# The last V ahead of wo, wo in five loads through four column tiles, K's pairs in one loop, one store

## The chip, the cores and the metric

The kernel runs on one core of a Trainium2 chip. The core has a matrix engine (PE; its weight loads are listed as PEld), a vector engine (DVE), a scalar engine (ACT), GpSimd (POOL) and a sync engine (SP) that here only issues transfers. Sixteen DMA engines move data between the chip's memory (DRAM) and the on-chip buffer; SP's loads stand in one queue, in the order in which SP issues them. The metric is the device time of one execution in microseconds; the time of a kernel is the median of its runs.

## What is computed

One step of a decoder for one token: attention over a long cache, a small feed-forward net, and a gate that mixes the two.

```python
q = (x @ wq).reshape(B, Sq, H, Dh)            # B = Sq = 1, D = 512, H = 32, Dh = 128
scores = einsum("bhqd,bhkd->bhqk", q, k_cache) * Dh ** -0.5      # Sk = 65536
p = softmax(scores, axis=-1)
o = einsum("bhqk,bhkd->bhqd", p, v_cache)
a = o.reshape(B, Sq, H * Dh) @ wo             # wo: 4096 x 512
b = (silu(x @ w_gate) * (x @ w_up)) @ w_down  # F = 1792
out = g * a + (1 - g) * b                     # g = sigmoid(sum(x * gate_w))
```

All tensors are bf16. K and V are 32 heads x 65536 positions x 128, 537 MB each; they are read once. wo is 4.2 MB.

## The kernel before

**Storage.** One buffer `mem` has 184 KB per partition, addressed in KB by `at(kb, n)`. A head's K and V come in halves z = 0 and 1 (in the load calls 0 and 1, in the names `a` and `z`) of 64 KB per partition, 8.39 MB each. K's first half lies at 32 to 96, its second at 0 to 64; V's first at 120 to 184, its second at 96 to 160. Halves overlap, so a half can be loaded when parts of the others have been used up. That is what the semaphores `ktdone` (pieces of K transposed by DVE) and `pvdone` (groups of value matmuls finished by PE) tell SP.

**The loop over heads.** DVE transposes K in sixteen pieces per head into two alternating buffers `kt` (lines 322, 415, 422). PE scores each piece against q with 32 small matmuls (`scores`, line 472), which are grouped in pairs of pieces, one for each buffer. The score row goes through a maximum (336, 547, 338, 549) and an exponential on ACT (288), and DVE puts it in the layout `pb` that the value matmuls need (331). One head behind, PE multiplies V by `pb` with 128 matmuls of 512 columns (line 525), in four groups: (0,0) with 40, (0,1) with 24, (1,0) with 40, (1,1) with 24. `psO` collects the head's row in 4 x 512; ACT scales it (280) and `turn()` brings it into a column (499), which ACT puts into `oTn` (282).

In one pass of the loop PE's order is: three pairs of K's first half in an inner loop, value group (0,0), the fourth pair written out, the turn of the last row, group (0,1), four pairs of K's second half, group (1,0), the maximum, group (1,1). SP's order is the next K first half, V first half, K second half, V second half, each behind a wait (lines 241 to 249). V's second half waits for group (0,0) (line 248).

**The end.** The last head's V isn't multiplied in the loop. After the last pass SP loads 31 of wo's 32 row blocks (line 251), then the last V in eight pieces (the list `tail`: place, first row, rows; a row is 128 x 128 values), then the block that is left twice: `wj` in the layout of the other blocks and `w31` with head 31's own rows (lines 260 and 261). PE multiplies the pieces of V as weights with a column of `pb` (`piece`, line 561, one matmul for each row, into a column `psW`). Between the first piece and the second, DVE has put the 31 finished heads into `amat`, one matmul (571) gathers them in wo's row order into `oR`, and 31 matmuls of 512 columns (576) add them to `psY`, which already holds the feed-forward branch. `psY` is copied to a row (440) and spread over `psZ` (584). When the last piece is done, DVE scales `psW` (442) and eight matmuls (600) add what is left, through two column tiles of two rows each. ACT copies the result (300), and ACT and SP store one half each.

Of the kernel before, what the change touches and what calls it, by code (L numbers as in the profile page):

```python
# [5 lines left out]
P = 128  # L6
KB = 512
PR = 32
# [13 lines left out]
def bass_gated_mix__mha_block_cached__swiglu_ffn__decode_kernel(  # L22
# [38 lines left out]
    tail = [(32, 0, 128), (0, 128, 128), (V0 + 24, 256, 128), (V0 + 64, 384, 64),  # L61
            (V0 + 80, 448, 32), (V0 + 56, 480, 16), (V0 + 60, 496, 12), (V0 + 63, 508, 4)]
    WOJ, WO31 = V0, V0 + 1

    with ExitStack() as ctx:
# [28 lines left out]
        hot = sb("hot", [P, 2, 2], F32)  # L94
# [10 lines left out]
        oR = sb("oR", [P, 32], BF16)  # L105
        w4 = sb("w4", [P, 2, 2, 2], BF16)
# [14 lines left out]
        names = ("x", "gw", "wq", "wg", "wu", "wd", "ka0", "ka", "kz", "va", "vz", "wo", "wj", "w31")  # L121
        d = {n: sem("d_" + n) for n in names}
        dt_ = [sem(f"d_t{i}") for i in range(len(tail))]
        s_ones = sem("s_ones")
# [6 lines left out]
        s_hot0 = sem("s_hot0")  # L131
        s_hot = sem("s_hot")
# [35 lines left out]
        s_oR = sem("s_oR")  # L168
        s_y = sem("s_y")
        s_yr = sem("s_yr")  # L170
        s_w = sem("s_w")
        s_w4 = sem("s_w4")
        s_wj = sem("s_wj")
# [3 lines left out]
        s_out2 = sem("s_out2")  # L177
# [12 lines left out]
        wj_dram = w_dram["wo"][:, 31 * D:32 * D]  # L190
        w31_dram = A_wo.rearrange("(h d) n -> h d n", d=Dh)[H - 1]
        WQ, WG, WU, WD, WO = V0, 0, 14, V0 + 64, 64
# [4 lines left out]
        wo_ap = at(WO, 32 * D).rearrange("p (j n) -> p j n", j=32)  # L197
        w2_ap = at(WOJ, 2 * D).rearrange("p (e c n) -> p e c n", e=2, c=4)
# [18 lines left out]
        ctx.callback(lambda: nc.sync.wait_ge(s_out2, 16))  # L217
        block = ctx.enter_context(nc.Block())

        @block.sync  # L220
        def _(sp):
            def load(kind, h, z):
                cache = A_k_cache if kind == "k" else A_v_cache
                sp.dma_start(at(place(kind, h, z), HR * Dh), kv_dram(cache, h)[z]).then_inc(d[kind + "az"[z]], 16)  # L224
# [12 lines left out]
            sp.wait_ge(ktdone, 2 * NP + NP // 2)  # L237
            load("k", 1, 1)
            sp.wait_ge(pvdone, 5)
            load("v", 0, 1)  # L240
            with nc.sync.Fori(0, H - 2) as i:
                sp.wait_ge(ktdone, i * (2 * NP) + (4 * NP - 4))
                load("k", i + 2, 0)
                sp.wait_ge(pvdone, i * 4 + 7)
                load("v", i + 1, 0)
                sp.wait_ge(ktdone, i * (2 * NP) + (4 * NP + NP // 2))
                load("k", i + 2, 1)
                sp.wait_ge(pvdone, i * 4 + 9)
                load("v", i + 1, 1)
            sp.wait_ge(ktdone, 2 * NP * H - NP)  # L250
            sp.dma_start(at(WO, 31 * D), w_dram["wo"][:, 0:31 * D]).then_inc(d["wo"], 16)
# [11 lines left out]
            sp.dma_start(out_dram[2:4, :], fin[32:34, :]).then_inc(s_out2, 16)  # L263

        @block.scalar
        def _(act):
# [31 lines left out]
            row_norm(H - 2)  # L298
            act.wait_ge(s_z4, 1)
            nc.scalar.copy(fin[0:34, :], psZ[0:34, 0:128]).then_inc(s_fin, 1)  # L300
            act.wait_ge(s_fin, 1)
            act.dma_start(out_dram[0:2, :], fin[0:2, :]).then_inc(s_out, 16)

        @block.vector
        def _(dve):
# [45 lines left out]
            link(nc.vector.memset(w4[:], 0.0))  # L351
            nc.vector.memset(psZ[0:64, 0:128], 0.0).then_inc(s_zz, 1)
            nc.vector.memset(hot[0:1, :, :], 0.0)
# [7 lines left out]
            nc.vector.memset(hot[0:1, :, :].rearrange("p a b -> p (a b)")[:, 0:4:3], 1.0).then_inc(s_hot, 1)  # L361
# [74 lines left out]
            nc.vector.tensor_copy(oR[:], psQ[:, 0, 0:32]).then_inc(s_oR, 1)  # L436
            diag = w4[:].rearrange("p e a b -> p e (a b)")[:, :, 0:4:3]
            nc.vector.tensor_copy(diag[:, 0, :], psQ[:, 0, 31:32].to_broadcast([P, 2])).then_inc(s_wj, 1)
            dve.wait_ge(s_y, 1)
            nc.vector.tensor_copy(yrow[0:1, :], psY[0:1, :]).then_inc(s_yr, 1)  # L440
            dve.wait_ge(s_w, 1)
            nc.vector.tensor_scalar(diag[:, 1, :], psW[:, 0:1].to_broadcast([P, 2]), LiG, None, ALU.mult).then_inc(s_w4, 1)

        @block.tensor
        def _(pe):
# [22 lines left out]
            def scores(b, col, j):  # L468
                for r in range(NG):
                    for je in range(4):  # L470
                        o = col + PR * b + 4 * r
                        last = nc.tensor.matmul(psS[:, o:o + 4] if j is None else psS[:, ds(j * (2 * PR) + o, 4)],  # L472
# [18 lines left out]
            for j in range(FC):  # L491
                last = nc.tensor.matmul(psY[0:1, :], guT[:, j:j + 1], wd_ap[:, j, :],
                                        start=(j == 0), stop=False)
# [3 lines left out]
            def turn():  # L497
                for i in range(4):
                    last = nc.tensor.matmul(psT[:, 0:1], orow[0:4, i * Dh:(i + 1) * Dh], ident[0:4, i:i + 1],  # L499
                                            start=(i == 0), stop=(i == 3))  # L500
                last.then_inc(s_pt, 1)

            nc.tensor.sem_inc(pvdone, 4)
            with nc.tensor.Fori(0, H) as i:
                n = i * (2 * NP)

                def pair(c, j):
                    for b in range(2):
                        if c == 0 and b == 0:
                            pe.wait_ge(s_qc, i + 1)  # L510
                        pe.wait_ge(ktdone, n + (c + b + 1) if j is None else n + j * 2 + (c + b + 1))
                        scores(b, PR * c, j)

                def pieces(z, c0, c1):
                    if c1 - c0 == 2:
                        pair(NP * z + c0, None)
                        return
                    with nc.tensor.Fori(0, (c1 - c0) // 2) as j:
                        pair(NP * z + c0, j)
# [11 lines left out]
                pieces(0, 0, NP - 2)  # L531
# [23 lines left out]
            def piece(n):  # L555
# [3 lines left out]
                for r in range(nr):  # L559
                    col = k_col[r0 + r]  # L560
                    last = nc.tensor.matmul(psW[:, 0:1], vt[:, r * Dh:(r + 1) * Dh], pb[:, col:col + 1],  # L561
                                            start=(r0 + r == 0), stop=(r0 + r == R - 1))
# [3 lines left out]
            turn()  # L566
            pe.wait_ge(s_pba, H)
            piece(0)
# [4 lines left out]
            pe.wait_ge(s_oR, 1)  # L573
            pe.wait_ge(d["wo"], 16)
            for j in range(31):
                last = nc.tensor.matmul(psY[0:1, :], oR[:, j:j + 1], wo_ap[:, j, :], start=False, stop=(j == 30))
            last.then_inc(s_y, 1)
            piece(1)
            pe.wait_ge(s_yr, 1)
            pe.wait_ge(s_hot, 1)  # L580
            pe.wait_ge(s_zz, 1)
            zt = [psZ[32 * (c // 2):32 * (c // 2) + 2, 0:128] for c in range(4)]
            for c in (0, 2, 1, 3):
                nc.tensor.matmul(zt[c], hot[0:1, c % 2, :], yrow[0:1, 128 * c:128 * c + 128],
                                 start=(c % 2 == 0), stop=False)
            pe.wait_ge(s_pbz, H)
            piece(2)
            piece(3)
            piece(4)
            piece(5)  # L590
            piece(6)
            piece(7).then_inc(s_w, 1)
            pe.wait_ge(s_wj, 1)
            pe.wait_ge(d["wj"], 16)
            for e in range(2):
                if e == 1:
                    pe.wait_ge(d["w31"], 16)
                    pe.wait_ge(s_w4, 1)
                for c in (0, 2, 1, 3):
                    last = nc.tensor.matmul(zt[c], w4[:, e, c % 2, :], w2_ap[:, e, c, :], start=False,  # L600
                                            stop=(e == 1 and c % 2 == 1))
# [29 lines left out]
```

## Time and profile before

| | us |
|---|---|
| median of 3 runs | 2513.8 (2513.74 to 2513.82) |
| span of the profiled execution | 2512.4 |
| PE busy | 1709.8 |
| DVE busy | 1411.8 |
| ACT busy | 64.6 |
| moved from DRAM | 1087.77 MB, 433 GB/s over the span |

The span is the time from the first to the last instruction of one profiled execution; the runs' times also hold what lies around it. A row of the timeline has the start in us from the start of the span, the length, engine, line, operation, output and inputs with their sizes, how many instructions are merged, and in brackets the idle time of that engine just before and what ended it. SPq and ACTq rows are the instructions that issue transfers. "Granted clock" is the matrix engine's clock as a share of its full speed.

### The profile page before, as it was taken

The page shows a single profiled execution, that of the slowest core. Times are in us where ns is not written, and L with a number is a line of the kernel's source. Part 1 is how long each engine was busy: PE and PEld are TensorE (multiplying, and loading weights), DVE is VectorE, ACT ScalarE, POOL GpSimd, SP SyncE. Part 2 cuts the span into 40 slices and gives each one's busy share as a digit, 9 for nine tenths or more (in the row PEclk, how much of TensorE's full clock was granted, in tenths as well). Part 3 has the DMA queues.
Part 4 walks back from the last instruction along what each step waited for, and adds up shares of the span by engine and source line. Part 5 has one row for each costly group of instructions (what it writes and reads, how often), then busy time and mean ns, then how long its engine had stood idle before and what let it go on. Part 6 is the DMA issues. An engine that isn't in the chain of part 4 may idle for free.

```text
span 2512.4 us, 51694 instructions
## 1 busy us (share of the span) xinstructions
PE 1709.8 (68%) x21624; PEld 978.8 (39%) x21624; DVE 1411.8 (56%) x1683; ACT 64.6 (3%) x195; POOL 0.2 (0%) x4
## 2 busy tenths in 40 slices
PE   4666766667667677676676766766767767677677
PEld 3334433333433344333443333343334333344334
DVE  4764565554655645646456555465564564645653
ACT  0000000000000000000000000000000000000000
POOL 0000000000000000000000000000000000000000
PEclk8667767777677677776776767767767677677677
DMA  9999999999999999999999999999999999999999
GB/s 420 436 434 434 434 435 434 434 434 434 434 434 434 434 434 434 434 434 434 434 434 434 434 434 434 434 434 434 434 434 434 434 434 434 435 434 434 434 435 402
DMA packets 20470, 1087.93 MB, mean 433 GB/s; under 512 B 2282, under 2 KB 2668, under 8 KB 2924
## 3 DMA queue, kind: packets, MB, share of 16 engines
q1 hardware_dynamic: 20452, 1087.78, 100.0%
q8 instruction: 9, 0.15, 0.0%
q14 instruction: 1, 0.01, 0.0%
q10 hardware_dynamic: 8, 0.00, 0.0%
HBM read 1087.77 MB, written 0.00 MB: 433 GB/s over the span
## 4 chain that ended last, share of the span: by engine, by line
DMA 70%; PE 27%; DVE 1%; issue 1%; SPq 0%; ACT 0%; DVEq 0%
DMA mem<-in_A_v_cache_dram 67%; PE psO L525 27%; DMA mem<-in_A_k_cache_dram 2%; DMA mem<-in_A_wo_dram 1%; DVE kt L322 1%; DMA mem<-in_A_wq_dram 0%; DVE kt L415 0%; SPq L224 0%; PE psM L456 0%; DVE pb L331 0%; PE psS L472 0%; PE psM L547 0%; DVE sm L336 0%; PE psZ L600 0%; PE psM L549 0%
## 5 line engine op out<-in xcount | busy, mean ns | idle before, releaser
L472 PE MATMUL psS<-qcur,kt 128*128 128x4 bf16 x16384 | 573.0, 169 | 728.3 <-DVE kt L415 414.2
L525 PE MATMUL psO<-mem,pb 128*4 128x512 bf16 x3968 | 1040.6, 428 | 32.9 <-DMA mem<-in_A_v_cache_dram 32.6
L472 PEld LDWEIGHTS psS<-qcur,kt 128*128 128x128 bf16 x16384 | 534.0, 105 | 791.9 <-issue 789.5
L422 DVE STREAM_TRANSPOSE kt<-mem 128x2048 uint32<-128x2048 uint32 x248 | 547.6, 2275 | 402.3 <-DMA mem<-in_A_k_cache_dram 402.3
L415 DVE STREAM_TRANSPOSE kt<-mem 128x2048 uint32<-128x2048 uint32 x248 | 551.3, 2280 | 240.3 <-DMA mem<-in_A_k_cache_dram 239.3
L525 PEld LDWEIGHTS psO<-mem,pb 128*4 128x4 bf16 x3968 | 359.4, 93 | 657.5 <-issue 238.4
L331 DVE COPY pb<-pa 32x64 bf16<-32x64 bf16 x1024 | 233.5, 228 | 15.1 <-ACT pa L288 1.5
L338 DVE TENSOR_REDUCE sc<-psM 1x1 f32<-1x128 f32 x32 | 8.9, 279 | 334.9 <-PE psM L547 334.9
L336 DVE TENSOR_REDUCE sm<-psS 128x1 f32<-128x512 f32 x32 | 22.1, 692 | 42.3 <-PE psS L472 42.3
L322 DVE STREAM_TRANSPOSE kt<-mem 128x2048 uint32<-128x2048 uint32 x16 | 35.4, 2277 | 17.0 <-DMA mem<-in_A_k_cache_dram 17.0
L286 ACT ACTIVATE sm<-psM 128x1 f32<-128x1 f32 x32 | 5.5, 171 | 1222.7 <-PE psM L549 1222.7
L282 ACT ACTIVATE oTn<-psT,gcol 128x1 f32 (+1 forms) x31 | 8.2, 264 | 1035.1 <-PE psT L499 1035.1
L499 PE MATMUL psT<-ident,orow 4*128 4x1 f32 x256 | 33.5, 248 | 0.5 <-ACT orow L280 0.5
L499 PEld LDWEIGHTS psT<-ident,orow 4*128 4x128 f32 x256 | 30.8, 186 | 1.2 <-ACT orow L280 0.6
L280 ACT ACTIVATE orow<-psO,sm 4x512 f32<-4x512 f32 x31 | 21.0, 677 | 130.3 <-PE psO L525 126.0
L288 ACT ACTIVATE pa<-psS,sm 128x512 bf16<-128x512 f32 x32 | 22.0, 687 | 1.0
L549 PE MATMUL psM<-sc,onesf 1*128 1x1 f32 x64 | 12.3, 259 | 11.9 <-DVE sc L338 11.9
L561 PE MATMUL psW<-pb,mem 128*128 128x1 bf16 x512 | 14.5, 164 | 5.2 <-DMA mem<-in_A_v_cache_dram 4.7
L549 PEld LDWEIGHTS psM<-sc,onesf 1*128 1x128 f32 x64 | 9.6, 186 | 21.5 <-DVE sc L338 21.5
L561 PEld LDWEIGHTS psW<-pb,mem 128*128 128x128 bf16 x512 | 13.9, 100 | 6.4 <-issue 4.2
L553 PEld LDWEIGHTS psM<-sm,onesf 128*128 128x128 f32 x64 | 9.7, 191 | 14.7 <-issue 13.5
L553 PE MATMUL psM<-sm,onesf 128*128 128x1 f32 x64 | 12.5, 264 | 1.1 <-ACT pa L288 1.1
(72 smaller groups left out, 94.0 us busy)
## 6 DMA issues: line engine op xcount, KB each, us to landing
mem<-in_A_v_cache_dram SPq DMA_DIRECT2D x3, 4096.0 KB, 29.4
mem<-in_A_k_cache_dram SPq DMA_DIRECT2D x2, 4096.0 KB, 38.7
mem<-in_A_wq_dram SPq DMA_DIRECT2D x1, 4096.0 KB, 12.3
mem<-in_A_wo_dram SPq DMA_DIRECT2D x1, 3968.0 KB, 36.7
mem<-in_A_v_cache_dram SPq DMA_DIRECT2D x1, 2048.0 KB, 31.2
mem<-in_B_w_gate_dram SPq DMA_DIRECT2D x1, 1792.0 KB, 16.0
mem<-in_B_w_up_dram SPq DMA_DIRECT2D x1, 1792.0 KB, 21.0
mem<-in_B_w_down_dram SPq DMA_DIRECT2D x1, 1792.0 KB, 24.7
```

The lines of the kernel that those rows point to most:

```text
L288: nc.scalar.activation(pa[:], psS[:], ACT.Exp, bias=nbias, scale=SCALE, accum_out=rsum).then_inc(expdone, 1)
L322: nc.vector.transpose(kt[:, i % 2, :].rearrange("p (j r t) -> p r j t", j=2, t=32), src.rearrange("p (r j t) -> p r j t", j=2, t=32)).then ...
L331: last = nc.vector.tensor_copy(dst, sr)
L336: nc.vector.reduce_max(mxs, psS[:], AX_X).then_inc(s_mx, 1)
L415: nc.vector.transpose(kt[:, c % 2, :].rearrange("p (j r t) -> p r j t", j=2, t=32), src.rearrange("p (r j t) -> p r j t", j=2, t=32)).then ...
L422: nc.vector.transpose(kt[:, c % 2, :].rearrange("p (j r t) -> p r j t", j=2, t=32), src.rearrange("p (r j t) -> p r j t", j=2, t=32)).then ...
L472: last = nc.tensor.matmul(psS[:, o:o + 4] if j is None else psS[:, ds(j * (2 * PR) + o, 4)], ktb[b][:, je // 2, r, :, je % 2], qcur[:, je, ...
L499: last = nc.tensor.matmul(psT[:, 0:1], orow[0:4, i * Dh:(i + 1) * Dh], ident[0:4, i:i + 1], start=(i == 0), stop=(i == 3))
L525: last = nc.tensor.matmul(psO[0:4, :], pb[:, k_col[256 * z + r]:k_col[256 * z + r] + 4], vt[:, r * Dh:(r + 4) * Dh], start=(z == 0 and par ...
L549: nc.tensor.matmul(amx, onesf[0:1, :], gm, start=True, stop=True).then_inc(s_ar, 1)
L553: nc.tensor.matmul(Lt, onesf[:], rsum, start=True, stop=True).then_inc(s_L, 1)
L561: last = nc.tensor.matmul(psW[:, 0:1], vt[:, r * Dh:(r + 1) * Dh], pb[:, col:col + 1], start=(r0 + r == 0), stop=(r0 + r == R - 1))
```

## The change

- The last pair of K's first half joins the other three in the inner loop, so value group (0,0) follows all four pairs. The fourth pair written out separately, and the branch between, are gone.
- The last V is loaded ahead of wo, in six pieces of 128, 128, 128, 72, 32 and 24 rows. wo is loaded after it, once, in five loads of 14, 9, 5, 3 and 1 row blocks, behind the wait for the last value group.
- The first piece of the last V is multiplied as the value matmuls in the loop are: `pb` as weights, V streaming past, 32 matmuls of 512 columns into `psO`. ACT copies the row out and a second turn adds it to `psW`, ahead of the last piece.
- All 32 heads are put in `amat`, the last one by four scalings on DVE when `psW` is complete; then one matmul gathers them and DVE copies them to `w1`.
- wo is multiplied by 128 matmuls of 128 columns, four for each row block, into four rows of `psZ` at partitions 0, 32, 64 and 96. The feed-forward branch is put there first, by four matmuls.
- ACT copies 97 partitions and stores all four rows in one transfer; SP's store is gone.

```diff
-    tail = [(32, 0, 128), (0, 128, 128), (V0 + 24, 256, 128), (V0 + 64, 384, 64),
-            (V0 + 80, 448, 32), (V0 + 56, 480, 16), (V0 + 60, 496, 12), (V0 + 63, 508, 4)]
+    tail = [(64, 0, 128), (32, 128, 128), (0, 256, 128), (V0 + 64, 384, 72), (V0 + 40, 456, 32), (V0 + 48, 488, 24)]
+    wo_rows = [14, 9, 5, 3, 1]
...
-            sp.wait_ge(ktdone, 2 * NP * H - NP)
-            sp.dma_start(at(WO, 31 * D), w_dram["wo"][:, 0:31 * D]).then_inc(d["wo"], 16)
-            need = {0: (ktdone, 2 * NP * H - 4), 1: (ktdone, 2 * NP * H), 2: (pvdone, 4 * H - 1)}
+            need = {0: (ktdone, 2 * NP * H - NP), 1: (ktdone, 2 * NP * H - 4), 2: (ktdone, 2 * NP * H),
+                    3: (pvdone, 4 * H - 1)}
...
             sp.wait_ge(pvdone, 4 * H)
-            sp.dma_start(at(WOJ, D), wj_dram).then_inc(d["wj"], 16)
-            sp.dma_start(at(WO31, D), w31_dram).then_inc(d["w31"], 16)
-            sp.wait_ge(s_fin, 1)
-            sp.dma_start(out_dram[2:4, :], fin[32:34, :]).then_inc(s_out2, 16)
+            j0 = 0
+            for n, nj in enumerate(wo_rows):
+                sp.dma_start(at(WO + j0, nj * D), w_dram["wo"][:, j0 * D:(j0 + nj) * D]).then_inc(dw_[n], 16)
+                j0 += nj
...
+            act.wait_ge(s_v0, 1)
+            nc.scalar.copy(orow[0:4, :], psO[0:4, :]).then_inc(s_or, 1)
             act.wait_ge(s_z4, 1)
-            nc.scalar.copy(fin[0:34, :], psZ[0:34, 0:128]).then_inc(s_fin, 1)
+            nc.scalar.copy(fin[0:97, :], psZ[0:97, 0:128]).then_inc(s_fin, 1)
             act.wait_ge(s_fin, 1)
-            act.dma_start(out_dram[0:2, :], fin[0:2, :]).then_inc(s_out, 16)
+            act.dma_start(out_dram, fin[0:97:32, :]).then_inc(s_out, 16)
...
+            nc.vector.tensor_copy(yrow[0:1, :], psY[0:1, :]).then_inc(s_yr, 1)
+            dve.wait_ge(s_w, 1)
+            for q in range(4):
+                w = slice(32 * q, 32 * q + 32)
+                last = nc.vector.tensor_scalar(amat[w, H - 1, q:q + 1], psW[w, 0:1], LiG[w], None, ALU.mult)
             last.then_inc(s_A, 1)
             dve.wait_ge(s_R, 1)
-            nc.vector.tensor_copy(oR[:], psQ[:, 0, 0:32]).then_inc(s_oR, 1)
...
+            nc.vector.tensor_copy(w1[:], psQ[:, 0, 0:32]).then_inc(s_w4, 1)
...
-                pieces(0, 0, NP - 2)
+                pieces(0)
                 with nc.tensor.If(i > 0):
                     pe.wait_ge(s_or, i)
                     pe.wait_ge(d["va"], i * 16)
                     pe.wait_ge(s_pba, i)
                     values(0, 0)
-                pieces(0, NP - 2, NP)
-                with nc.tensor.If(i > 0):
-                    turn()
+                    turn().then_inc(s_pt, 1)
                     values(0, 1)
-                pieces(1, 0, NP)
+                pieces(1)
...
+                    if n == 0:
+                        last = nc.tensor.matmul(psO[0:4, :], pb[:, col:col + 4], vt[:, r * Dh:(r + 4) * Dh],
+                                                start=(r == 0), stop=(r == nr - 4))
...
-            piece(0)
+            piece(0).then_inc(s_v0, 1)
+            piece(1)
+            pe.wait_ge(s_yr, 1)
+            pe.wait_ge(s_zz, 1)
+            zt = [psZ[32 * c:32 * c + 1, 0:128] for c in range(4)]
+            for c in range(4):
+                nc.tensor.matmul(zt[c], onesf[0:1, 0:1], yrow[0:1, 128 * c:128 * c + 128], start=True, stop=False)
+            pe.wait_ge(s_pbz, H)
+            piece(2)
+            piece(3)
+            piece(4)
+            pe.wait_ge(s_or, H + 1)
+            turn(psW, False, False)
+            piece(5).then_inc(s_w, 1)
             pe.wait_ge(s_A, 1)
             pe.wait_ge(s_b0, 1)
             nc.tensor.matmul(psQ[:, 0, 0:32], amat[:].rearrange("p h q -> p (h q)"), bmat[:],
                              start=True, stop=True).then_inc(s_R, 1)
...
+            pe.wait_ge(s_w4, 1)
+            j0 = 0
+            for n, nj in enumerate(wo_rows):
+                pe.wait_ge(dw_[n], 16)
+                for j in range(j0, j0 + nj):
+                    for c in range(4):
+                        last = nc.tensor.matmul(zt[c], w1[:, j:j + 1], wo_ap[:, j, c, :], start=False, stop=(j == 31))
+                j0 += nj
             last.then_inc(s_z4, 1)
```

More of the change, by code (lines that the diff above doesn't have):

```diff
@@ L93, in bass_gated_mix__mha_block_cached__swiglu_ffn__decode_kernel @@
         onesf = sb("onesf", [P, 128], F32)
-        hot = sb("hot", [P, 2, 2], F32)
         sc = sb("sc", [P, 8], F32)
@@ L104, in bass_gated_mix__mha_block_cached__swiglu_ffn__decode_kernel @@
         bmat = sb("bmat", [P, 32], BF16)
-        oR = sb("oR", [P, 32], BF16)
-        w4 = sb("w4", [P, 2, 2, 2], BF16)
+        w1 = sb("w1", [P, 32], BF16)
         fin = sb("fin", [P, 128], BF16)
@@ L119, in bass_gated_mix__mha_block_cached__swiglu_ffn__decode_kernel @@
         gm = sc[0:1, 5:6]
-        names = ("x", "gw", "wq", "wg", "wu", "wd", "ka0", "ka", "kz", "va", "vz", "wo", "wj", "w31")
+        names = ("x", "gw", "wq", "wg", "wu", "wd", "ka0", "ka", "kz", "va", "vz")
         d = {n: sem("d_" + n) for n in names}
         dt_ = [sem(f"d_t{i}") for i in range(len(tail))]
+        dw_ = [sem(f"d_w{i}") for i in range(len(wo_rows))]
         s_ones = sem("s_ones")
@@ L130, in bass_gated_mix__mha_block_cached__swiglu_ffn__decode_kernel @@
         s_unit = sem("s_unit")
-        s_hot0 = sem("s_hot0")
-        s_hot = sem("s_hot")
         s_z = sem("s_z")
@@ L167, in bass_gated_mix__mha_block_cached__swiglu_ffn__decode_kernel @@
         s_R = sem("s_R")
-        s_oR = sem("s_oR")
-        s_y = sem("s_y")
         s_yr = sem("s_yr")
         s_w = sem("s_w")
+        s_v0 = sem("s_v0")
         s_w4 = sem("s_w4")
-        s_wj = sem("s_wj")
         s_z4 = sem("s_z4")
@@ L176, in bass_gated_mix__mha_block_cached__swiglu_ffn__decode_kernel @@
         s_zz = sem("s_zz")
-        s_out2 = sem("s_out2")
         s_out = sem("s_out")
@@ L189, in bass_gated_mix__mha_block_cached__swiglu_ffn__decode_kernel @@
         }
-        wj_dram = w_dram["wo"][:, 31 * D:32 * D]
-        w31_dram = A_wo.rearrange("(h d) n -> h d n", d=Dh)[H - 1]
-        WQ, WG, WU, WD, WO = V0, 0, 14, V0 + 64, 64
+        WQ, WG, WU, WD, WO = V0, 0, 14, V0 + 64, V0
         wq_ap = at(WQ, Dc * H * Dh).rearrange("p (c n) -> p c n", c=Dc)
@@ L196, in bass_gated_mix__mha_block_cached__swiglu_ffn__decode_kernel @@
         wd_ap = at(WD, FC * D).rearrange("p (c n) -> p c n", c=FC)
-        wo_ap = at(WO, 32 * D).rearrange("p (j n) -> p j n", j=32)
-        w2_ap = at(WOJ, 2 * D).rearrange("p (e c n) -> p e c n", e=2, c=4)
+        wo_ap = at(WO, 32 * D).rearrange("p (j c n) -> p j c n", j=32, c=4)
         ktb = [kt[:, b, :].bitcast(BF16).rearrange("p (j r m e) -> p j r m e", j=2, r=NG, e=2) for b in range(2)]
@@ L216, in bass_gated_mix__mha_block_cached__swiglu_ffn__decode_kernel @@
         ctx.callback(lambda: nc.scalar.wait_ge(s_out, 16))
-        ctx.callback(lambda: nc.sync.wait_ge(s_out2, 16))
         block = ctx.enter_context(nc.Block())
@@ L350, in _ @@
             link(nc.vector.memset(amat[:], 0.0))
-            link(nc.vector.memset(w4[:], 0.0))
-            nc.vector.memset(psZ[0:64, 0:128], 0.0).then_inc(s_zz, 1)
-            nc.vector.memset(hot[0:1, :, :], 0.0)
+            nc.vector.memset(psZ[:, 0:128], 0.0).then_inc(s_zz, 1)
             nc.vector.memset(ident[:], 0.0)
@@ L360, in _ @@
             link(last)
-            nc.vector.memset(hot[0:1, :, :].rearrange("p a b -> p (a b)")[:, 0:4:3], 1.0).then_inc(s_hot, 1)
             link(nc.vector.transpose(kt[:, 1, 0:1024], kt[:, 0, 0:1024]))
@@ L433, in _ @@
                 last = nc.vector.tensor_copy(amat[32 * q:32 * q + 32, 0:H - 1, q], oTn[32 * q:32 * q + 32, 0:H - 1])
+            nc.vector.tensor_copy(yrow[0:1, :], psY[0:1, :]).then_inc(s_yr, 1)
[3 more added lines that the diff above has]
+                last = nc.vector.tensor_scalar(amat[w, H - 1, q:q + 1], psW[w, 0:1], LiG[w], None, ALU.mult)
             last.then_inc(s_A, 1)
             dve.wait_ge(s_R, 1)
[L436 to L442, printed above, removed]
+            nc.vector.tensor_copy(w1[:], psQ[:, 0, 0:32]).then_inc(s_w4, 1)
         @block.tensor
@@ L471, in scores @@
                         o = col + PR * b + 4 * r
-                        last = nc.tensor.matmul(psS[:, o:o + 4] if j is None else psS[:, ds(j * (2 * PR) + o, 4)],
+                        last = nc.tensor.matmul(psS[:, ds(j * (2 * PR) + o, 4)],
                                                 ktb[b][:, je // 2, r, :, je % 2],
@@ L492, in _, with turn @@
                 last = nc.tensor.matmul(psY[0:1, :], guT[:, j:j + 1], wd_ap[:, j, :],
-                                        start=(j == 0), stop=False)
+                                        start=(j == 0), stop=(j == FC - 1))
             last.then_inc(s_b, 1)
             pe.wait_ge(s_unit, 1)
-            def turn():
+            def turn(to=psT, first=True, final=True):
                 for i in range(4):
-                    last = nc.tensor.matmul(psT[:, 0:1], orow[0:4, i * Dh:(i + 1) * Dh], ident[0:4, i:i + 1],
-                                            start=(i == 0), stop=(i == 3))
-                last.then_inc(s_pt, 1)
+                    last = nc.tensor.matmul(to[:, 0:1], orow[0:4, i * Dh:(i + 1) * Dh], ident[0:4, i:i + 1],
+                                            start=(first and i == 0), stop=(final and i == 3))
+                return last
             nc.tensor.sem_inc(pvdone, 4)
@@ L510, in pair, with pieces @@
                             pe.wait_ge(s_qc, i + 1)
-                        pe.wait_ge(ktdone, n + (c + b + 1) if j is None else n + j * 2 + (c + b + 1))
+                        pe.wait_ge(ktdone, n + j * 2 + (c + b + 1))
                         scores(b, PR * c, j)
[L514 to L519, printed above, removed]
+                def pieces(z):
+                    with nc.tensor.Fori(0, NP // 2) as j:
+                        pair(NP * z, j)
                 def values(z, part):
@@ L558, in piece @@
                 vt = at(kb, nr * Dh)
-                for r in range(nr):
+                for r in range(0, nr, 1 if n else 4):
                     col = k_col[r0 + r]
-                    last = nc.tensor.matmul(psW[:, 0:1], vt[:, r * Dh:(r + 1) * Dh], pb[:, col:col + 1],
-                                            start=(r0 + r == 0), stop=(r0 + r == R - 1))
+                    if n == 0:
+                        last = nc.tensor.matmul(psO[0:4, :], pb[:, col:col + 4], vt[:, r * Dh:(r + 4) * Dh],
+                                                start=(r == 0), stop=(r == nr - 4))
+                    else:
+                        last = nc.tensor.matmul(psW[:, 0:1], vt[:, r * Dh:(r + 1) * Dh], pb[:, col:col + 1],
+                                                start=(n == 1 and r == 0), stop=(r0 + r == R - 1))
                 return last
             pe.wait_ge(s_or, H)
-            turn()
+            turn().then_inc(s_pt, 1)
             pe.wait_ge(s_pba, H)
-            piece(0)
+            piece(0).then_inc(s_v0, 1)
[12 more added lines that the diff above has]
+            piece(5).then_inc(s_w, 1)
             pe.wait_ge(s_A, 1)
@@ L572, in _ @@
                              start=True, stop=True).then_inc(s_R, 1)
[L573 to L601, printed above, removed]
+            pe.wait_ge(s_w4, 1)
[6 more added lines that the diff above has]
+                j0 += nj
             last.then_inc(s_z4, 1)
```

1 line of the change is left out of this document (removed).

## The prediction

> **What bounds the kernel now.** I read the page first, for what runs without a pause.
>
> ```profile
> span 2512.4 us, 51694 instructions
> ...
> DMA  9999999999999999999999999999999999999999
> GB/s 420 436 434 434 434 435 434 434 434 434 434 434 434 434 434 434 434 434 434 434 434 434 434 434 434 434 434 434 434 434 434 434 434 434 435 434 434 434 435 402
> ...
> q1 hardware_dynamic: 20452, 1087.78, 100.0%
> ...
> mem<-in_A_wq_dram SPq DMA_DIRECT2D x1, 4096.0 KB, 12.3
> ```
>
> The transfers never pause: 434 GB/s in nearly every slice, 420 in the first and 402 in the last. 1087.78 MB at 434 GB/s are 2506.4 us of the 2512.4. So time can only be won by moving fewer bytes, at the start, or in the few microseconds at the end; it can be lost wherever a transfer is issued too late. The last row gives the price of a load that finds the queue empty: 4096 KB are 4.19 MB, 9.66 us at 434 GB/s, and it took 12.3, so about 2.6 us lie around it.
>
> Then the end of the chain of waits (start, length, what):
>
> ```profile
> 2433.30 27.91 DMA mem<-in_A_v_cache_dram
> ...
> 2479.22 30.75 DMA mem<-in_A_wo_dram
> 2509.97 0.14 issue
> 2510.11 0.62 PE psZ L600 x8
> 2510.74 0.02 issue
> 2510.76 0.26 ACT fin L300
> ```
>
> After the transfers only eight small matmuls, one copy and the store remain, 2.4 us. The span is 2512.4 and the runs' median 2513.8; 1.4 us lie outside the span, and I add them at the end.
>
> Third, the timeline of the last pass through the head loop, for what releases the V loads:
>
> ```profile
> 2416.06 8.89 DVE L415 STREAM_TRANSPOSE kt<-mem 128x2048 uint32<-128x2048 uint32 x4
> ...
> 2420.70 1.14 PE L472 MATMUL psS<-qcur,kt 128*128 128x4 bf16 x32 [1.01 <-DVE kt L415]
> 2422.56 10.58 PE L525 MATMUL psO<-mem,pb 128*4 128x512 bf16 x40 [0.72 <-DMA mem<-in_A_v_cache_dram]
> ...
> 2433.07 1.75 PE L472 MATMUL psS<-qcur,kt 128*128 128x4 bf16 x64
> 2433.30 0.33 SPq L224 DMA_DIRECT2D mem<-in_A_v_cache_dram  x1
> ...
> 2433.85 0.34 SPq L251 DMA_DIRECT2D mem<-in_A_wo_dram  x1
> ...
> 2435.73 7.03 PE L525 MATMUL psO<-mem,pb 128*4 128x512 bf16 x24
> ...
> 2444.41 1.13 PE L472 MATMUL psS<-qcur,kt 128*128 128x4 bf16 x32 [1.65 <-DVE kt L422]
> ```
>
> The 40 value matmuls start as V's first half lands, and their end issues V's second half (2433.30). The last pair of K pieces is scored behind them, long after its transposes were ready (2416.06 + 8.89 = 2424.95).
>
> **The change, part by part.**
>
> *Bytes.* Before, row block 31 of wo is loaded twice in two layouts (wj and w31, 128 KB each, beside the 31 blocks). Afterwards wo is loaded once: 128 KB less, 0.131 MB / 434 GB/s = 0.30 us. **-0.30**, since nothing else sets the time.
>
> *Sizes of the last loads.* Eleven tail loads stay eleven (wo, eight of V, wj, w31; then six of V, five of wo). The smallest were 4, 3, 1, 1, 1 KB per partition, now 5, 3, 1.
>
> ```profile
> 2505.00:2508.00 3.00, 2.44 (x86) 2.28 (x83) 0.00 (x0) 0.00 (x0) 0.00 (x0) 0.50 0.99 396
> 2508.00:2510.00 2.00, 1.38 (x40) 1.13 (x37) 0.03 (x1) 0.00 (x0) 0.00 (x0) 0.50 0.61 217
> ```
>
> In these windows (last three columns: granted clock, DMA share, GB/s) the small loads run at 396 GB/s: 3 us x 38/434 = 0.26 us lost. The last two, at a share of 0.61, are the ragged end of the sixteen engines, which stays. Of the 0.26 the change may win all or nothing: **-0.1**, with ends -0.26 and 0, since two of five small loads go.
>
> *K's pairs in one loop.* This touches all heads. The last pair moves ahead of the first 40 value matmuls, so these wait for the eighth transpose (2424.95) and the scoring of its piece (1.14, and some 0.4 to leave the loop, as 2420.70 + 1.14 = 2421.84 stands to 2422.56 less the 0.72 that was spent on V): they start near 2426.5 and not at 2422.56, **4.0 us later**. What is queued behind them: the turn of the last head's row, the 24 further value matmuls, and on SP the issue of V's second half. The PE side is covered: the two value groups no longer have 1.75 us of scoring between them, so the 24 end near 2445 where they ended at 2442.8, and the next scoring starts at 2444.4; at most half a microsecond, and where it isn't made up it counts against the same cover. The DMA side is the one that counts:
>
> ```profile
> DMA to landing us min/median/max: 26.7/28.4/49.1
> ```
>
> This is the row of the loads that line 224 issues, 125 in all. Each moves 8.39 MB, 19.3 us at 434 GB/s. The second half of V in the chain above took 27.91, so it stood behind others for 8.6 us; the load with the least took 26.7, 7.4 us. Less the 2.6 us of an empty queue, the cover is 6.0 us there and 4.8 in the worst head. A delay of 4.0 leaves 2.0 and 0.8: **0 us**, lower end 0 (a queue that is full can't gain). How long the 40 matmuls take doesn't change the sum as long as the clock behaves as before:
>
> ```profile
> 2422.50:2426.20 3.70, 3.64 (x9) 1.10 (x10) 3.63 (x8) 0.00 (x0) 0.00 (x0) 0.50 1.06 461
> 2426.20:2433.20 7.00, 7.00 (x37) 2.68 (x36) 2.56 (x12) 0.00 (x0) 0.00 (x0) 1.00 1.04 449
> ```
>
> Nine matmuls ran at half clock in the first 3.7 us, the others at full clock. After the change they again follow a stretch of scoring with gaps, so the same is expected. [...]
>
> *The last V ahead of wo.* SP's order changes: the first 4 MB of the last V take wo's place at 2433.85 (moved by the same 4.0), each later piece moves up by one, and wo's five loads are issued last, behind the wait for the last value matmuls, where wj was (2479.22). What lies ahead of them in the queue then is the end of V: it lands 9.7 us before the transfers end, near 2500.2, which is 21 us after the issue. No gap: **0**. Bounded: if it did run dry it would cost the 2.6 us of an empty queue, but 21 us of cover stand against it.
>
> *PE's tail.*
>
> ```profile
> 2480.01 1.05 PE L499 MATMUL psT<-ident,orow 4*128 4x1 f32 x8 [0.51 <-ACT orow L280]
> ...
> 2480.99 3.36 PE L561 MATMUL psW<-pb,mem 128*128 128x1 bf16 x128
> ...
> 2484.93 8.17 PE L576 MATMUL psY<-mem,oR 128*1 128x512 bf16 x31 [0.28 <-DVE oR L436]
> ...
> 2493.04 3.36 PE L561 MATMUL psW<-pb,mem 128*128 128x1 bf16 x128
> ...
> 2499.93 3.55 PE L561 MATMUL psW<-pb,mem 128*128 128x1 bf16 x128 [3.00 <-DMA mem<-in_A_v_cache_dram]
> ...
> 2509.97 0.22 DVE L442 TENSOR_SCALAR w<-psW,sm 128x2 bf16<-128x2 f32 x1 [16.15 <-PE psW L561]
> ```
>
> Piece 0 becomes 32 matmuls of 512 columns: 10.58/40 = 0.264 each, 8.5 us in place of 3.36. From 2480.99 that ends at 2489.5; the 8.17 us of wo that followed are gone. Piece 1: 3.4. The four matmuls that bring in the other branch: 0.6. Piece 2 (3.5) then ends near 2497, pieces 3 and 4 (104 rows at 3.36/128 = 0.026, 2.7) near 2500, the second turn (1.05) 2501. Piece 5, landed at 2500.2, 24 rows, 0.7, ends at 2501.7. Four scalings on DVE at 0.22, the gather by one matmul and its copy (0.4 together), and w1 is ready near 2503. The first load of wo, 14 blocks of 0.30 us, lands 4.2 us after V, at 2504.4. So the new chain through DVE, PE and DVE is hidden by 1.4 us; without that cover PE has still the later loads to catch up in. **0**.
>
> *wo through four column tiles.* 128 matmuls of 128 columns. At half clock 512 columns cost 3.7/9 = 0.41, so 128 cost about 0.107. No row shows four tiles at once. The eight of line 600, on two tiles at a granted 0.50, took 0.62 with a wait for w31 in the middle; one after the other they would need 8 x 0.107 = 0.86, so two tiles do overlap. With four, a row block costs 0.107 against 0.30 of transfer and PE waits for each load; with two, 0.21, still below 0.30; with none, 0.43. I take four, because nothing in the instructions differs but the offset of 32. After the last load there are four matmuls where there were eight in two steps, and no scaling at 2509.97: **-0.1**; ends -0.3 and, with two tiles only, +0.9: 32 x 0.21 = 6.9 us from 2504.4 end at 2511.3, where 2510.4 was.
>
> [...]
>
> *One store.*
>
> ```profile
> SPq L217 <- DMA out_dram<-fin: 0.6, 1, 0.6
> ...
> 2511.04 0.33 SPq L263 DMA_DIRECT2D out_dram<-fin  x1
> 2511.05 0.26 ACTq L302 DMA_DIRECT2D out_dram<-fin  x1
> ```
>
> The two issue together, SP's takes 0.07 longer, and SP waits 0.6 at the end. Without it ACT's alone decides: **-0.1**, between -0.6 and 0. The copy ahead of it spans 97 partitions for 34, same 128 columns: nothing.
>
> **The sum.** -0.30 - 0.1 - 0.1 - 0.1 = -0.6; span 2511.8; with the 1.4 outside, **2513.2**. Its own range, by the ends of the terms: 2512.6 to 2514.4 (the two-tile case with no other gain but the bytes).
>
> **The rivals.**
>
> *A. V's second half comes too late* (slower). Place: SP's issue behind the 40 value matmuls, every head. It decides from a delay over 4.8 us. [...] Every further microsecond of delay is about 31 us. For it: little cover is left, and PE is half idle just before. Against: the clock did rise in the first 3.7 us in the row above, and a short wait first strikes the engines that run ahead.
>
> *B. The column tiles don't overlap.* 128 x 0.107 = 13.7 us from 2504.4 end at 2518.1, 7.7 late: **2521**. Against: line 600.
>
> *C. PE comes late to wo.* If piece 0 runs at half clock throughout (32 x 0.41 to 0.43, 13.7 us), PE is 5.2 behind, w1 is ready at 2508.2, and 32 x 0.107 = 3.4 us end at 2511.6, 1.2 late: **2514.4**. Against: piece 0 is a dense stream that follows a dense stream.
>
> *D. Nothing but order changes:* the ragged end of the engines swallows the bytes and the store: **2513.8**.
>
> **How the numbers follow.** Forecast 0.68, D 0.12, A 0.10, C 0.05, B 0.03, something else 0.02. About 0.2% (5 us) is what a measurement of this kernel can tell from no change; forecast, C and D lie inside it. Slower: A and B, 0.13. Faster needs 5 us, and at 434 GB/s the bytes alone leave no more than 6: 0.01. The range 2512.5 to 2515.0 takes in C, D and the ends of the terms.
>
> **What would show it.** Right: 434 GB/s in all middle slices; line 525's first group some 4 us later against the transposes and loads of line 224 with a minimum near 22.7 us from issue to landing; PE waiting for each of wo's five loads; the four last matmuls about 0.4 us after the last landing. Wrong: gaps in the DMA share once per head (A); wo's matmuls back to back past the last landing, at 0.1 us each (B) or starting behind 2506 (C).

## The result, and the profile after

The changed kernel takes 2526.53 us (median of 6 runs, 2522.63 to 2537.15) against 2513.81 (2513.74 to 2513.95): 1.0056 of the time before, 95% interval 1.0042 to 1.0070. Forecast were 2513.2 and a range up to 2515.0. The runs of the kernel before agree within 0.2 us; those of the changed one differ by 14.5.

The page of the changed kernel, its rows on the transfers and the shares of its chain of waits:

```profile
span 2528.9 us, 52299 instructions
...
DMA  9999999999999999999999999999999999999999
GB/s 420 430 431 431 431 431 431 430 431 433 431 430 431 430 429 431 427 435 433 432 431 431 432 436 428 426 431 432 432 432 431 431 431 431 441 431 432 434 432 385
...
q1 hardware_dynamic: 20448, 1087.64, 99.8%
...
DMA 75%; DVE 14%; issue 9%; PE 1%; SPq 0%; DVEq 0%; ACT 0%
```

The DMA row still shows full busy digits, but the GB/s row has fallen from 434 to about 431 in nearly every slice. The loss is spread over the whole run, not put at the end. The bytes are 0.14 MB fewer, as the change says. The last row of the view shares out the chain of waits. Before it was

```profile
DMA 70%; PE 27%; DVE 1%; issue 1%; SPq 0%; ACT 0%; DVEq 0%
```

The chain now runs by way of DVE's transposes (14%, 1% before) and hardly through PE's value matmuls (1%, 27% before). It says which work the next issue stands behind, not what that costs.

The timeline of the last pass through the loop, the rows that answer to those of before (PE's lines 458 and 508 were 472 and 525, DVE's 402 was 415, SP's 213 was 224):

```profile
2430.65 8.89 DVE L402 STREAM_TRANSPOSE kt<-mem 128x2048 uint32<-128x2048 uint32 x4
...
2439.68 1.16 PE L458 MATMUL psS<-qcur,kt 128*128 128x4 bf16 x32 [1.00 <-DVE kt L402]
...
2441.19 11.20 PE L508 MATMUL psO<-mem,pb 128*4 128x512 bf16 x40 [0.35 <-issue]
...
2452.56 0.33 SPq L213 DMA_DIRECT2D mem<-in_A_v_cache_dram  x1
```

Everything stands where the prediction put it: the 40 value matmuls start 1.65 us after the eighth transpose (2430.65 + 8.89 = 2439.54), and V's second half is issued right behind them. The row on the loads of line 213:

```profile
DMA to landing us min/median/max: 22.9/28.5/49.3
```

The shortest way from issue to landing fell from 26.7 to 22.9; "near 22.7" was forecast. So the delay was right, and what it costs was not.

**Where the time went.** The sixteen landings of each load can be read from the semaphore events in the trace. Call *lead* the time from the issue of V's second half to the first of the sixteen landings of the load ahead of it. Before, a load's first landing follows that of the load ahead by 19.31 to 19.33 us in every head. Afterwards V's second halves, and nearly they alone, take longer:

```
sum over 31 heads of what the median landing takes beyond 19.32 us
                      before   changed
V second half           1.0      13.0
V first half           -0.6       0.5
K first half           -0.3       0.6
K second half           0.0       1.0

changed kernel: lead of V's second half, heads, mean loss of the head (us)
0 to 1      3 heads   1.04
1 to 1.5    4 heads   0.97
1.5 to 2    8 heads   0.42
2 to 2.5    6 heads   0.19
2.5 to 3    7 heads   0.11
3 to 4      3 heads   0.25
```

The four rows of the changed kernel add up to 15.1 us; the profiled run took 17.1 longer than the median before. Before, the lead was 6.5 us on average and 5.7 at least; now 2.1 and 0.8. What happens to an engine shows in its packets of 64 KB, which take 2.42 us each in an unbroken stream. Two heads of the changed kernel, from the trace's packet records:

```
issue of V's second half       1056.05     508.09
lead                              0.84       3.81
first of its packets starts    1056.77     511.56   (511.56: right behind the load ahead)
the next from                  1057.02
of the first 16, lengthened      14          0
longest of them                   3.41       2.42
```

With a short lead the first packets start 0.72 to 0.97 us after the issue, and the first round of packets takes up to 3.41 us. A lengthened packet counts as busy for the whole of its time, so the DMA row (9 in all 40 slices) hides this and the GB/s row (431 for 434) shows it. Why these packets take longer was not tested.

The end of the chain of waits, for the terms of the tail:

```profile
2494.31 30.13 DMA mem<-in_A_wo_dram
...
2524.48 0.70 PE psZ L577 x19
2525.18 0.96 issue
2526.14 0.70 PE psZ L577 x17
...
2526.87 0.27 ACT fin L290
```

PE waits for wo's first three loads as they land (idle 0.39, 0.99 and 0.39 us ahead of them, put down to their DMA). The 0.96 us ahead of the last seventeen matmuls are put down to "issue", not to a load: the first of them still belongs to the third load, which landed at 2524.44. By 2526.14 the last two loads were there as well (2525.81 and 2526.08). Seventeen matmuls of 128 columns take 0.70 us at the granted 0.50, where one after the other they would need, by the estimate of 0.107 each, 17 x 0.107 = 1.8 us: the four tiles overlap.

### The profile page after: what moved, and what is told of

Same layout as the page of the kernel before. It is cut to its first block, busy times and chain, and to the rows that moved or that the text cites. A ratio compares the mean times of both kernels' runs of the same rounds, so it can differ in the third digit from the quotient of the medians.

```text
span 2528.9 us, 52299 instructions
## 1 busy us (share of the span) xinstructions
PE 1704.2 (67%) x21625; PEld 996.0 (39%) x21625; DVE 1412.4 (56%) x1682; ACT 65.1 (3%) x196; POOL 0.2 (0%) x4
## 4 chain that ended last, share of the span: by engine, by line
DMA 75%; DVE 14%; issue 9%; PE 1%; SPq 0%; DVEq 0%; ACT 0%
DMA mem<-in_A_k_cache_dram 72%; DVE kt L402 7%; DVE kt L409 6%; DMA mem<-in_A_wo_dram 1%; PE psO L508 1%; DMA mem<-in_A_v_cache_dram 1%; DVE kt L312 1%; DMA mem<-in_A_wq_dram 0%; SPq L213 0%; PE psM L442 0%; DVE pb L321 0%; DVEq L407 0%; PE psS L458 0%; PE psZ L577 0%; DVEq L400 0%
## 5 line engine op out<-in xcount | busy, mean ns | idle before, releaser
L458 PE MATMUL psS<-qcur,kt 128*128 128x4 bf16 x16384 | 597.4, 170 | 748.7 <-DVE kt L402 476.4
L508 PE MATMUL psO<-mem,pb 128*4 128x512 bf16 x3968 | 1009.0, 419 | 32.3 <-DMA mem<-in_A_v_cache_dram 22.1
L458 PEld LDWEIGHTS psS<-qcur,kt 128*128 128x128 bf16 x16384 | 556.0, 106 | 803.4 <-issue 803.3
L508 PEld LDWEIGHTS psO<-mem,pb 128*4 128x4 bf16 x3968 | 353.9, 91 | 630.8 <-issue 203.6
L321 DVE COPY pb<-pa 32x64 bf16<-32x64 bf16 x1024 | 233.6, 228 | 15.1 <-ACT pa L276 1.5
L530 PE MATMUL psM<-sc,onesf 1*128 1x1 f32 x64 | 12.3, 259 | 11.9 <-DVE sc L328 11.9
L528 PE MATMUL psM<-ident,sm 128*1 128x128 f32 x64 | 12.4, 276 | 0.8 <-DVE sm L326 0.8
## 6 DMA issues: line engine op xcount, KB each, us to landing
mem<-in_A_wq_dram SPq DMA_DIRECT2D x1, 4096.0 KB, 12.2
mem<-in_A_v_cache_dram SPq DMA_DIRECT2D x1, 2304.0 KB, 24.6
mem<-in_A_wo_dram SPq DMA_DIRECT2D x1, 1792.0 KB, 26.7
```

The lines of the kernel that those rows point to most:

```text
L321: last = nc.vector.tensor_copy(dst, sr)
L458: last = nc.tensor.matmul(psS[:, ds(j * (2 * PR) + o, 4)], ktb[b][:, je // 2, r, :, je % 2], qcur[:, je, :], start=(je == 0), stop=(je == 3))
L508: last = nc.tensor.matmul(psO[0:4, :], pb[:, k_col[256 * z + r]:k_col[256 * z + r] + 4], vt[:, r * Dh:(r + 4) * Dh], start=(z == 0 and par ...
L530: nc.tensor.matmul(amx, onesf[0:1, :], gm, start=True, stop=True).then_inc(s_ar, 1)
```

## The experiments

Two theories stand against each other. *Late issue*: all of the loss comes from SP's issue of V's second half behind the 40 value matmuls. *The rest*: the new end, or PE's new order in the loop, costs the time.

**e1: the old order of K's pairs, the new end.**

```diff
...
-                pieces(0)
+                pieces(0, 0, NP - 2)
                 with nc.tensor.If(i > 0):
...
                     values(0, 0)
+                pieces(0, NP - 2, NP)
+                with nc.tensor.If(i > 0):
                     turn().then_inc(s_pt, 1)
```

> The changed kernel with K's pairs in the old order: three pairs, the 40 value matmuls, the fourth pair; the whole new end stays. Late-issue theory (V's second half of every head is issued about 4 us too late, all else costs less than 1 us): 2513.0 to 2514.6, and the loads of the loop again take at least 26.7 us from issue to landing. Rival (the new end or its order of loads costs the time): stays above 2520.

Measured: 2513.92 us, 1.0001 of before (0.9991 to 1.0010). The row of its loads:

```profile
DMA to landing us min/median/max: 26.7/28.4/49.1
```

The new end costs nothing, and gains nothing either.

**e2: the kernel before with K's pairs in one loop, nothing else.**

```diff
-                pieces(0, 0, NP - 2)
+                pieces(0, 0, NP)
                 with nc.tensor.If(i > 0):
...
                     values(0, 0)
-                pieces(0, NP - 2, NP)
-                with nc.tensor.If(i > 0):
                     turn()
```

> The kernel before with one edit, K's four pairs in one loop. Late-issue theory: as slow as the changed kernel, 2522 to 2532, with a shortest time from issue to landing near 23 us. Rival (the new end): 2513.8.

Measured: 2529.47 us, 1.0066 (1.0050 to 1.0083). This one edit carries the whole loss.

```profile
DMA to landing us min/median/max: 22.9/28.3/49.2
```

**e4: PE untouched, only the issue later.**

```diff
...
-                sp.wait_ge(pvdone, i * 4 + 9)
+                sp.wait_ge(s_dl, i + 2)
                 load("v", i + 1, 1)
...
+                        if z == 0 and part == 1 and m == 4:
+                            last.then_inc(s_dl, 1)
```

> The kernel before with its own order on PE; only SP's wait for V's second half is moved from the end of the 40 value matmuls to the fifth of the 24 that follow, about 4.2 us later. Late-issue theory: 2522 to 2532, though PE does exactly what it did. Rival (PE's order): 2513.8.

Measured: 2524.26 us (2516.02 to 2533.31), 1.0038 (1.0023 to 1.0054). PE does what it did before, and the loss is there. The median stands in the expected interval; of the ten runs four lie below it and one above. So PE's order is not needed for the loss.

**e3: the new order, but something in the queue ahead of the late issue.**

`load_v1` loads the first 24 KB of each partition with 0 and the other 40 KB with 1.

```diff
...
                 load("k", i + 2, 1)
+                sp.wait_ge(pvdone, i * 4 + 8)
+                load_v1(i + 1, 0)
                 sp.wait_ge(pvdone, i * 4 + 9)
-                load("v", i + 1, 1)
+                load_v1(i + 1, 1)
...
-                    pe.wait_ge(d["vz"], i * 16)
+                    pe.wait_ge(d["vz"], i * 32)
```

> The changed kernel with K's pairs in one loop as they are, but V's second half in two loads: its first 24 KB per partition, which overlap nothing that is still in use, are issued right behind K's second half, the other 40 KB where the whole was. That puts 7.2 us of transfer in the queue ahead of the late issue. Late-issue theory: 2513.0 to 2515. Rival (PE's new order itself holds up the heads, whatever the queue holds): 2522 or more.

Measured: 2516.52 us, 1.0010 (1.0000 to 1.0020). Ten of the 12.7 us come back with PE's order as it is, so the late issue is the cause. It missed the interval by 1.5 and is 2.6 slower than e1. The two parts land 7.27 and 12.09 us after what is ahead of them, 19.36 for 19.32, so every load that is added to the full queue costs about 0.04 us, 1.3 in 31 heads. Another 0.7 lie at the end: the copy starts 1.09 us after the last landing, 0.42 in e1, with an idle stretch of 0.85 put down to "issue" ahead of the last seventeen matmuls, as in the changed kernel. The last 0.6 lie outside the span and stay unexplained.

**e5, e10 and e6: how much lead is enough.** Three more delays in the kernel before, made as in e4: behind the fourth pair, behind the first and behind the sixteenth of the 24 matmuls.

> The kernel before, V's second half waiting for the fourth pair to be scored too, some 1.75 us later; PE unchanged. The late-issue theory with a threshold (a load must be issued 2.4 us before the first of the sixteen engines lands the load ahead; before had 6.4 on average, this leaves 4.7) says 2513.9, no loss. Rival (every microsecond of delay costs in proportion, as 4.2 us cost 10 to 13): 2518 to 2519.

> The kernel before with V's second half waiting for the first of the 24 matmuls, about 3 us later than before; PE unchanged. The lead is then about 3.4 us on average and 2.6 in the tightest head. With a threshold near 2.5 us: 2513.8 to 2516. If every head with a lead under 4 us loses: 2518 or more.

> The kernel before, V's second half waiting for the sixteenth of the 24 matmuls, some 6.7 us later than before; PE unchanged. Threshold theory: the issue comes about when the first engine lands the load ahead, so each of 31 heads loses the whole way of a load into an idle engine, 1.9 to 2.5 us: 2570 to 2592. Rival (the loss saturates near 1 us, the lengthening of the first packets seen in the changed kernel): 2540 to 2550.

Measured: 2513.89 us, 1.0000 (0.9991 to 1.0010); 2514.47 us, 1.0004 (0.9994 to 1.0013); 2556.37 us, 1.0171 (1.0154 to 1.0188). The first two came as the theory of a threshold has it; the third missed both of its ranges. The shortest ways from issue to landing are 24.6, 23.8 and 21.7 us.

With the leads from the traces this is one curve. Leads and losses are those of the profiled run, so its own time stands beside them:

```
kernel    mean lead  least lead  loss of V's second halves, 31 heads  profiled run  median
before       6.5        5.7                  1.0                         2513.8     2513.8
e5           4.7        3.5                 -0.1                         2513.9     2513.9
e10          3.7        2.8                  0.8                         2514.2     2514.5
e4           2.3        1.2                 12.2                         2527.3     2524.3
e2           2.3        0.7                 12.7                         2527.8     2529.5
changed      2.1        0.8                 13.0                         2530.9     2526.5
e6           0.7       -1.9                 40.3                         2555.7     2556.4
```

In the traces a mean delay of 1.7 us (e5) costs nothing, one of 2.9 (e10) 0.6 and one of 4.0 to 4.1 (e2, e4, the changed kernel) 10 to 16. So the cost isn't in proportion to the delay: it sets in where the lead falls below about 2.5 us.

e6 lies between what the two theories of its expectation gave. Its delay was as planned: on average V's second half is issued 18.1 us after V's first half has landed, 11.1 before. But the lead fell by 5.8 and not by 6.9, because the sixteen landings ahead now lie 0.6 us apart where they lay 1.7 apart. The loss of a head is 40.3/31 = 1.3, in line with the changed kernel's 1.04 for leads under 1. Lead and loss add up to 1.9 to 2.1 us in every head of e6, also in the one that was issued 1.9 us behind the first landing and lost 3.8. With a lead under 1 us, then, a head loses what its lead lacks of about 2 us; the changed kernel's three such heads add up to 1.9 each.

**e7: packets half as long at the same late place.**

```diff
...
+                if kind == "v" and z == 1:
+                    for c0 in (0, HR * Dh // 2):
+                        sp.dma_start(at(VZ, HR * Dh)[:, c0:c0 + HR * Dh // 2],
+                                     kv_dram(cache, h)[z][:, c0:c0 + HR * Dh // 2]).then_inc(d["vz"], 16)
+                    return
...
```

> The changed kernel with V's second half issued at the same late place in two loads of 32 KB per partition, so that an engine's packets are half as long. If the lead that a load needs is one packet of read-ahead (2.42 us for 64 KB), half the packet needs half the lead and the loss shrinks to 2 to 6 us: 2516 to 2520, the second load's own 1.4 us among it. If the lead is a fixed way from issue to engine and from memory, the loss stays: 2523 to 2530.

Measured: 2530.76 us, 1.0060 (1.0043 to 1.0077), just above the range for a fixed way. Packets of half the length win nothing, so the lead isn't one packet of read-ahead. A fixed way from the issue to the engine fits; no run shows it by itself.

**e9: the smallest cover.** e3 with 8 KB in place of 24.

> As e3, but the early part of V's second half is only 8 KB per partition, 2.4 us of transfer. The needed lead read from the heads of the changed kernel is about 2.5 us ahead of the first landing, and the changed kernel has 2.1 on average, 0.8 at least. With 2.4 more nearly all heads have enough: as fast as e3, 2516 to 2518 (each load that is added costs 0.045 us, 31 times). If it takes the 24 KB to be safe (a lead of 5 us or more): 2519 or more.

Measured: 2516.71 us, 1.0011 (1.0001 to 1.0020), as expected and as e3; the lead in the trace is 4.9 us on average, 4.0 at least. 2.4 us of transfer ahead of the late issue are all that was missing.

**e8: e1 with two stores.**

```diff
...
+            sp.wait_ge(s_fin, 1)
+            sp.dma_start(out_dram[2:4, :], fin[64:97:32, :]).then_inc(s_out2, 16)
...
-            act.dma_start(out_dram, fin[0:97:32, :]).then_inc(s_out, 16)
+            act.dma_start(out_dram[0:2, :], fin[0:33:32, :]).then_inc(s_out, 16)
```

> The kernel of e1 (K's pairs in the old order, the new end) with the store again in two halves, from ACT and SP. In the profile of e1 the one store of four rows took 0.61 us to issue and 1.7 us from the end of the copy to the end of the span. If the one store costs this: the end comes 0.3 us sooner, 2513.5 to 2513.7, the fastest so far. Rival (the store is the same either way): 2513.9.

Measured: 2514.89 us (2514.00 to 2515.80), 1.0004 (0.9994 to 1.0013): not faster, and outside both values that were expected. Five runs lie at 2514.0 to 2514.3 and five at 2515.4 to 2515.8. The profiled one is of the slower five; there the last engine lands wo at 2511.44, 2510.11 in e1, so at least that run is slower by its transfers and not by its stores. From the end of the copy to the end of the span it took 1.9 us, 1.7 in e1. Its stores:

```profile
2512.15 0.62 SPq L255 DMA_DIRECT2D out_dram<-fin  x1
2512.16 0.60 ACTq L296 DMA_DIRECT2D out_dram<-fin  x1
```

Two rows at partitions that lie 32 apart take 0.60 and 0.62 us to issue, as four did (0.61); two rows side by side took 0.26 and 0.33 in the kernel before. So in these runs the step between the partitions goes with the longer issue, and not their number.

No version is faster than the kernel before.

## Why the prediction was wrong

- *Bound and bytes*: right. The transfers set the end; 0.14 MB fewer were moved.
- *The delay of V's second half*: right, "4.0 us later". The 40 matmuls start 4.05 us behind V's landing (2441.19 against 2437.14 in the trace), and over the 31 heads V's second half is issued 4.1 us later against that landing. One term was read wrongly: 2422.56 less 0.72 is 2421.84 itself, so the rows quoted give nothing for leaving the loop; after the change the trace has 0.35.
- *The cover*: **the step that failed.** "Less the 2.6 us of an empty queue, the cover is 6.0 us there and 4.8 in the worst head." The 2.6 came from the first load of the kernel, counted to its last landing. What a full queue needs is counted to the first engine that runs dry: about 2.5 us of lead before its landing, and that comes 1.7 us before the last one. So 4.2 of the 8.6 and 7.4 us were no cover; 4.4 and 3.2 were left, and the delay was 4.1 on average: the issue came 13.8 to 16.6 us after V's landing, 10.3 to 11.9 before. Of 31 heads 21 had a lead under 2.5. The term for K's pairs, put at 0 us, measured 12.7 here and 15.5 alone in e2.
- *Rival A* had the place and the mechanism, at a chance of 0.10, with a decision point of 4.8 us that was too late: the loss is there at 4.1 on average. It needs nothing of the clock: e4 leaves PE as it was and loses as much at the same delay (12.2 and 13.0 us in 31 heads). Its sign, gaps in the DMA share, didn't show: the share stays 1.00 in the loop and only the rate falls (430 to 433 GB/s between 100 and 2474 us, 433 to 435 before).
- *"A short wait first strikes the engines that run ahead"*: true, but no reason for no cost. In 31 heads the last landings lost 13.2 us in all, the first ones 11.6. In the head of 121.08 an engine got its first packet of the new load only at 124.30, 3.2 us after the issue. One that is served late falls behind the others, and the transfer ends with the last. That this is the whole reason was not tested.
- *The order of V and wo at the end*: right, no gap.
- *Four column tiles*: right. Rival B falls: 128 took 3.58 us in e1 at a granted 0.50, 28 ns each. (The 0.107 us for one alone is an estimate, a quarter of the 0.43 us that lie between matmuls of 512 columns at 0.50 in the kernel before, whose weight loads start at 2422.95, 2423.37, 2423.80; 3.7/9 would give 0.103. Nothing hangs on it.)
- *The tail's sum*: -0.6 was forecast, e1 shows nothing. The end of e1's timeline:

```profile
2494.96 3.57 PE L551 MATMUL psW<-pb,mem 128*128 128x1 bf16 x128 [1.29 <-issue]
...
2501.44 1.44 PE L551 MATMUL psW<-pb,mem 128*128 128x1 bf16 x48 [2.90 <-issue]
...
2506.89 3.58 PE L582 MATMUL psZ<-mem,w 128*1 128x128 bf16 x128 [0.28 <-DVE w L428]
2510.53 0.27 ACT L290 CAST fin<-psZ 97x128 bf16<-97x128 f32 x1 [21.67 <-PE psZ L582]
2510.82 0.61 ACTq L292 DMA_DIRECT2D out_dram<-fin  x1
```

The copy starts at 2510.53 where it was 2510.76: bytes, sizes and matmuls gave 0.23, not 0.5. The store, forecast at -0.1, took it back: 1.7 us from the end of the copy to the end of the span (2512.5), 1.3 before. *Rival C* was half right in its place: PE came to wo at 2506.89 and not 2503, but because of two idle stretches put down to "issue", not of piece 0, whose 32 matmuls took 7.07 us, about the 6.94 that 32 such matmuls took before at a granted 1.00. It caught up at 28 ns a matmul.

## What to carry to other kernels

Where one queue of transfers sets the time, the number to watch is the lead of each issue over the first engine to finish the load ahead; here 3.5 us in every head were free and 2.1 on average cost 13 us in 31 heads. Before a compute step is moved ahead of the point that frees a buffer, add up the delay against that lead in the tightest head, and price an unknown latency by the first engine to run dry, not by the time of a whole load. If the order must stay, a small load that overwrites nothing still in use, queued ahead of the late one, buys the lead back, here for 0.04 us a piece in the queue.

## What was not expected of the hardware

- The busy share hid most of the loss; only GB/s showed it (431 for 434). Of the 16.5 us by which the span grew, the packets of an engine account on average for 11.9 by taking longer (they fill 2524.0 of 2528.9 us, before 2512.1 of 2512.4), and idle time for 4.6.
- In e6 the first packet came 0.96 to 1.16 us after the start of the issue, which itself takes 0.33; in the heads with 0.96 that is 0.63 from the end of the issue. A head with a lead under 1 us still loses what it lacks of about 2, and its first packets are longer as well (3.41 us for 2.42 in the head of 1056.05).
- A store from partitions with a step of 32 issues in 0.60 to 0.62 us, one from neighbours in 0.26 to 0.33.
- PE's idle stretches in e1 (1.29 and 2.90 us) stand 128 matmuls with their weight loads, 256 instructions, apart. In the changed kernel's end two such stretches (3.10 and 0.68 us) stand 128 matmuls apart too. What PE waits for in them was not tested.
- Open: why runs of the same late kernel differ by up to 17 us (e4, 2516.0 to 2533.3), where kernels with enough lead agree within 1.4 us or, at the wider spread of e8 and e10, about 2.
